# Two-input operations moved to VectorE and weight roundings to GpSimd in a fused attention and two-MoE kernel

## The chip, the cores and the metric

One Trainium2 chip, one core of it. The metric is the device time of the program in microseconds (us); for one core it is that core's time. Engines: TensorE (PE, with its weight loads as PEld), VectorE (DVE), ScalarE (ACT), GpSimd (POOL), and SyncE (SP), which issues all loads and stores.

## The reference

```python
def reference(**kwargs):
    attn_out = _attn_ref(**attn_kwargs)      # q, k, v: (4, 8, 576, 64); s: (4, 8, 576)
    B, H, S, D = attn_out.shape
    x = np.ascontiguousarray(attn_out.transpose(0, 2, 1, 3)).reshape(B * S, H * D)
    x = _moe_ref(x=x, **moe_kwargs)
    return _moe2_ref(x=x, **moe2_kwargs)
```

Attention is causal, with scores scaled by 1/8 and lowered by the running sum of max(s, 0) between key and query, then a softmax and the product with v. The first MoE is max(max(x w1, x w2), x w3) w_out with 2304 tokens, 512 columns in and out and 768 hidden ones. The second is ((x w_a) * (x w_b)) w_out with 1536 hidden columns. The second result is the output.

## The kernel before, in words

Every large product is made in three parts from split operands. An operand t is rounded into a high part (`rnd`, a copy into the type fp32r) and a low part t - high (`sub`, or `tt` with subtract); then high*high + high*low + low*high goes through TensorE. So each tensor that feeds TensorE costs one rounding (one input) and one subtraction (two inputs in SBUF) on ScalarE, VectorE or GpSimd; which engine does which is written out by hand at each place. In the code "A" is ScalarE, "V" VectorE and "P" GpSimd.

The stages overlap at their edges:

- **Attention and first MoE** (to some 520 us). Eight steps (4 batches, query rows up to 256 and above it), four pairs of heads in each. The first three steps ("plain") use unsplit operands for scores and values; the others split q, k, v and the probabilities. The products of the first MoE for one step (`moe1_units`, `gate` at L623 and `outp` at L650) are put between the attention pieces of later steps, so TensorE has one or the other. Its 24 weights of 128x512 come as 64-bit numbers and are made into fp32 by one ScalarE and three VectorE integer operations (`load_w`, L235 to L240), then split: rounding on ScalarE, subtraction on GpSimd (called at L244 and L245, recorded at L79 and L90). They are loaded over the first 1.8 steps. `vsplit` (v), `x_pair` (attention's result, Xh and Xl) and `gate` (hidden values, hh and hl) each end in a subtraction on GpSimd.
- **Second MoE, gates** (some 520 to 818 us). Both of its products use a seven-product scheme over 2x2 blocks: `a_side` and `b_side` make the sums of blocks and split seven operands each, and `Unit.prod` makes products 1, 2, 6, 5, 7, 4, 3 and adds them up from the PSUM banks X, Y and Z with ScalarE copies (L1087, L1091, L1093) and VectorE sums. Products 4 and 3 of a unit are made inside the next one (`emit`). There are 12 chunks of weights (`load_w2`, tiles wh and wl, each of two memory places) and 3 token blocks (`x2_part`, tiles xh and xl): 36 units of 42 matmuls of 384 columns. `load_w2` makes fp32 into wval, then does 4 VectorE sums, 7 ScalarE roundings and 7 GpSimd subtractions of 256 columns. `x2_part` for blocks 1 and 2 does 4 sums and 7 splits of 768 columns. The product a*b is made on VectorE for one half (`c21`) and on GpSimd for the other (`done`), and goes to HBM as hT.
- **Output** (from 818 us). Nine units of 256 tokens, 126 matmuls of 256 columns each (`outs`). `prep_wo` splits w_out once (tile wo; woh and wol of 128x1536: 4 sums, 7 roundings, 7 subtractions), `load_h` reads a block of hT into hraw with four loads, and `prep_h` does 4 sums and 7 splits of 128x768 into slots.

The order on each engine is made by a scheduler from the program's order and priorities: `tc.high_priority(n)` lets what stands in it come as if it stood n places earlier. Each engine then works its list in order, and so does SP with its loads and stores. Tiles lie in pools that are stacked from the left or the right end of SBUF; a pool that is laid over a released one waits for the old tiles' last readers, tile by tile. In the second MoE the left stack is wop (w_out, and before it the raw x of blocks 1 and 2), tmpA (raw weights, s, u), xr1 (x operands of block 1), wB (weights of odd chunks), xr2 (block 2), over the weights of the first MoE. In the output stage tmpB lies over tmpA, and lB (slots, l3, h7, l7, h4, l4, the second hraw) over the rest.

Of the kernel before, what the change touches and what calls it, by code (L numbers as in the profile page):

```python
# [27 lines left out]
def kernel(  # L28
# [44 lines left out]
    def f(ap):  # L73
        return ap.bitcast(F32)
# [148 lines left out]
    def load_w(raw, src, hi, lo):  # L223
# [5 lines left out]
        else:  # L229
# [13 lines left out]
            val = f(L)  # L243
        rnd("A", hi, val)  # L244
        sub("P", lo, val, f(hi))  # L245

# [115 lines left out]
    def vsplit(R, vn):  # L362

        Vs = ap_.tile([P, 5, 4, D], F32R, tag="Vs", bufs=1, name="Vs")
        nb = 5 if R else 2
        v_ = vn.rearrange("p b (h d) -> p b h d", h=2)
        hi, lo = Vs[:, :nb, 0:4:3, :], Vs[:, :nb, 1:3, :]
        rnd("P", hi, v_)
        sub("P", lo, v_, f(hi))
        return Vs  # L370
# [218 lines left out]
    def x_pair(R, p, pa, pb, Xh, Xl):  # L589
# [8 lines left out]
        rnd("A", Xh[:, p, :], xf[:, :n])  # L598
        sub("P", Xl[:, p, :], xf[:, :n], f(Xh[:, p, :]))

# [7 lines left out]
    def moe1_units(R, b, X):  # L608
# [4 lines left out]
        def gate(m, g):  # L613
# [19 lines left out]
            if g == 2:  # L633
                if m == 0:
                    st["hh"] = mp.tile([P, MF, N1], F32R, tag="hh", bufs=1, name="hh")
                    st["hl"] = mp.tile([P, MF, N1], F32R, tag="hl", bufs=1, name="hl")
                rnd("A", st["hh"][:, m, :n], hf)
                sub("P", st["hl"][:, m, :n], hf, f(st["hh"][:, m, :n]))

# [308 lines left out]
    def hilo(eng, hi, lo, src):  # L948
        rnd("A", hi, src)
        tt(eng, lo, src, f(hi), ALU.subtract)  # L950

# [74 lines left out]
    def load_x0():  # L1026
        for k in range(KH):
            q = rA.tile([P, 4, 1, TB], F32, tag="xt", bufs=1, name="xt")
            x2_part(0, k, k + 1, q, "PV")

# [12 lines left out]
    wop = lpool("wop")  # L1043
    xt12 = wop.tile([P, 2, 4, KH, TB], F32, tag="wo", name="xt12")
    tmpA = lpool("tmpA")
    rawp.append(tmpA)
    xr[1] = lpool("xr1")
    wpool[1] = lpool("wB")
# [54 lines left out]
    def gates(c, sb):  # L1103
# [20 lines left out]
        def done(t):  # L1124
            tt("P", t[1], t[0], t[1], ALU.mult)
            nc.sync.dma_start(hT[c * P : (c + 1) * P, t0 : t0 + TB], t[1])
# [38 lines left out]
    for n, (c, sb) in enumerate(order):  # L1165
        extra = []
        if n < 2:
            extra.append(lambda n=n: x2_part(n + 1, 0, KH, xt12[:, n], "VP"))
        done_c = [cc for cc in range(MF2) if (cc, NSB - 1) in order[:n]]
# [9 lines left out]
    xr[2].release()  # L1179
    wpool[1].release()  # L1180
    xr[1].release()
    tmpA.release()
    xr[0].release()
# [14 lines left out]
    hraw = [rB2.tile([P, MF2, 2 * P], F32, name="hraw0")]  # L1198
    wo_tiles(rB2, ("h1", "l1", "h2", "l2", "h3"))
    tmpB = lpool("tmpB")  # L1200
    obs = [tmpB.tile([P, DM], F32, name=f"ob{i}") for i in range(6)]
    tmpB.tile([P, 256], F32, name="pad2")
    lB = lpool("lB")
    slots = [lB.tile([P, KO, P], F32R, name=f"slot{i}") for i in range(18)]
    wo_tiles(lB, ("l3", "h7", "l7", "h4", "l4"))
    hraw.append(lB.tile([P, MF2, 2 * P], F32, name="hraw1"))
    NSLOT = len(slots)

    def prep_wo():
        eng = dict(zip((1, 2, 3, 6, 5, 7, 4), "VVPVVPV"))  # L1210
        b_side(
            [wo32[0][:, s] for s in range(4)],
            lambda i, q: hilo(eng[i], wot[f"h{i}"], wot[f"l{i}"], q),
        )

# [14 lines left out]
    def prep_h(j):  # L1230
        r = hraw[j % 2]
        hi, lo = {}, {}
        eng = dict(zip((1, 2, 4, 6, 5, 7, 3), "PVPVPVV"))

# [37 lines left out]
    NPR = len(porder)  # L1272
    with tc.high_priority(260):
        load_h(0)
    with tc.high_priority(160):
        prep_h(0)
    with tc.high_priority(100):
        prep_wo()
        load_h(1)
# [8 lines left out]

    lB.release()
    tmpB.release()  # L1290
    wop.release()
    ps_w.release()
# [89 lines left out]
```

## Time and profile before

| | |
|---|---|
| Runs | 973.07, 974.68, 978.18 us (median 974.68) |
| The profiled execution | 976.56 us, span 974.8 us |
| Mean granted TensorE clock | 0.986 of full speed |
| Busy share | TensorE 95%, weight loads 89%, VectorE 67%, ScalarE 49%, GpSimd 45% |
| Instructions of VectorE, ScalarE, GpSimd | 1349, 1068, 479 |

The span is what the trace covers; the profiled execution's own time is 1.8 us longer. Matmuls are pipelined, so a matmul's own duration is longer than the distance to the next one, and the rate of a stretch is read from its count. In a timeline line the columns are start, duration, engine, line and operation, written tile and read tiles, and in brackets how long the engine had been idle before and what ended that. Where a helper issues the operations, all have its line (L946 for `tt`, L79 to L86 for `rnd`, L90 for `sub`), so the tiles tell them apart.

### The profile page before, as it was taken

To read this page: it belongs to the slowest core of one execution; us is meant where nothing else is said; L and a number is where in the kernel's file an instruction comes from. 1 tells how busy PE (TensorE), PEld (TensorE's weight loads), DVE (VectorE), ACT (ScalarE), POOL (GpSimd) and SP (SyncE) were. 2 spreads that over 40 slices of the span, in tenths; PEclk is the share of its full clock that TensorE was granted. 3 is DMA by queue.
4 is the path that set the end of the run, shared out by engine and by line. 5 is a ranking of instruction groups with operands and counts; after the bars stand their busy time and mean duration, and the time that the engine had idled before them with its cause. 6 is when DMAs were issued, how large, how long until landed. Compare 5 with 4: busy or idle time off the path is not lost. (4 is left out here: it accounts for less than half of the span.)

```text
span 974.8 us, 17135 instructions
## 1 busy us (share of the span) xinstructions
PE 921.4 (95%) x6158; PEld 868.6 (89%) x6158; DVE 652.1 (67%) x1349; ACT 476.4 (49%) x1068; POOL 443.1 (45%) x479
## 2 busy tenths in 40 slices
PE   5999999999999999999998799898989997699998
PEld 4676689999999999999988698898989997699998
DVE  5899533686567766666574967766655567978774
ACT  4776643666556665566434434333333344345442
POOL 5676423355453455445364533333333435643431
PEclk9999999999999999999999799999999998899999
DMA  5655233212322141310325224444332133243531
GB/s 168 190 164 184 72 98 106 77 43 75 96 81 78 42 126 56 107 42 2 98 77 200 75 93 163 151 129 143 114 113 100 49 117 119 65 156 106 172 109 44
DMA packets 55213, 102.36 MB, mean 105 GB/s; under 512 B 5736, under 2 KB 39432, under 8 KB 55128
## 3 DMA queue, kind: packets, MB, share of 16 engines
q1 hardware_dynamic: 55128, 101.26, 33.0%
q8 instruction: 49, 0.80, 0.3%
q14 instruction: 36, 0.29, 0.1%
HBM read 77.29 MB, written 23.94 MB: 104 GB/s over the span
## 5 line engine op out<-in xcount | busy, mean ns | idle before, releaser
L623 PE MATMUL g<-Xh,hg 128*128 128x256 f32 (+1 forms) x576 | 172.1, 302 | 2.2 <-ACT hf L629 1.5
L623 PE MATMUL g<-Xl,hg 128*128 128x256 f32 (+1 forms) x576 | 172.7, 301 | 0.4 <-DVE Xl L90 0.4
L623 PE MATMUL g<-Xh,lg 128*128 128x256 f32 (+1 forms) x576 | 171.9, 300 | 0.0
L623 PEld LDWEIGHTS g<-Xh,hg 128*128 128x128 f32 x576 | 108.0, 189 | 5.3 <-ACT hf L629 1.7
L1058 PE MATMUL X<-xh,wh 128*128 128x384 f32 x288 | 100.5, 349 | 12.3 <-ACT s L1087 5.7
L623 PEld LDWEIGHTS g<-Xl,hg 128*128 128x128 f32 x576 | 109.0, 189 | 2.5 <-issue 1.0
L623 PEld LDWEIGHTS g<-Xh,lg 128*128 128x128 f32 x576 | 108.8, 189 | 2.3 <-issue 1.5
L946 POOL TENSOR_TENSOR wl<-wval,wh 128x256 fp32r<-128x256 f32 x84 | 69.6, 848 | 80.8 <-ACT wh L79 72.7
L1058 PE MATMUL X<-xl,wh 128*128 128x384 f32 x288 | 97.9, 340 | 0.0
L1058 PE MATMUL X<-xh,wl 128*128 128x384 f32 x288 | 97.8, 341 | 0.0
L946 POOL TENSOR_TENSOR slot<-hraw,slot 128x768 fp32r<-128x768 f32 x27 | 56.5, 2095 | 71.3 <-ACT slot L79 66.8
L946 POOL TENSOR_TENSOR u<-s,u 128x384 f32<-128x384 f32 x36 | 43.7, 1213 | 95.8 <-issue 63.9
L1058 PE MATMUL X<-woh,slot 128*128 128x256 f32 x432 | 83.7, 285 | 2.9 <-DVE slot L946 1.2
L79 ACT ACTIVATE slot<-hraw 128x768 fp32r<-128x768 f32 x63 | 52.3, 845 | 57.5 <-DVE hraw L946 48.1
L406 POOL TENSOR_SCALAR P<-P,rs 128x128 f32<-128x128 f32 (+2 forms) x80 | 47.1, 593 | 72.5 <-DVE rs L402 62.2
L1058 PEld LDWEIGHTS X<-woh,slot 128*128 128x128 f32 x432 | 69.4, 192 | 4.2 <-DVE slot L946 1.4
L1058 PEld LDWEIGHTS X<-xh,wh 128*128 128x128 f32 x288 | 54.7, 190 | 19.4 <-ACT s L1087 7.2
L946 DVE TENSOR_TENSOR hraw<-hraw 128x768 f32<-128x768 f32 x36 | 50.4, 1401 | 25.6 <-POOL slot L946 25.0
L632 DVE TENSOR_TENSOR hf<-g,hf 128x256 f32<-128x256 f32 (+1 forms) x96 | 43.5, 453 | 27.2 <-PE g L623 21.6
L1058 PE MATMUL X<-wol,slot 128*128 128x256 f32 x216 | 60.9, 283 | 0.0
L90 POOL TENSOR_TENSOR hl<-hf,hh 128x256 fp32r<-128x256 f32 (+1 forms) x48 | 41.5, 865 | 42.2 <-ACT hh L79 41.9
L650 PE MATMUL o<-hh,ho 128*128 128x256 f32 (+1 forms) x192 | 56.3, 302 | 1.7 <-DVE hf L632 1.3
(185 smaller groups left out, 2693.2 us busy)
## 6 DMA issues: line engine op xcount, KB each, us to landing
hT<-u SPq DMA_DIRECT2D x72, 192.0 KB
hraw<-hT SPq DMA_DIRECT2D x36, 384.0 KB
wraw<-in_moe_w_dram SPq DMA_DIRECT2D x18, 512.0 KB
wraw<-in_moe_w_out_dram SPq DMA_DIRECT2D x18, 512.0 KB
qvraw<-in_qv_dram SPq DMA_DIRECT2D x12, 640.0 KB
kraw<-in_kT_dram SPq DMA_DIRECT2D x24, 288.0 KB
wraw<-in_moe_w_a_dram SPq DMA_DIRECT2D x12, 512.0 KB
wraw<-in_moe_w_b_dram SPq DMA_DIRECT2D x12, 512.0 KB
```

The costliest lines, as they stand in the source:

```text
L79: nc.scalar.activation(o, i, AF.Copy, scale=scale)
L90: e.tensor_tensor(o, a, b, op=ALU.subtract)
L406: nc.gpsimd.tensor_scalar(pt[:, c0:c1], pt[:, c0:c1], rs[:, g : g + 1], 1.0, op0=ALU.mult, op1=ALU.mult,)
L623: nc.tensor.matmul(ps[:, :n], w[:, kk, :], x[:, kk, :], start=(i == 0), stop=(i == len(mm) - 1),)
L632: nc.vector.tensor_tensor(hf, ps[:, :n], hf, op=ALU.max)
L650: nc.tensor.matmul(ps[:, :n], w[:, c, :], x[:, m, :n], start=(i == 0), stop=(i == len(mm) - 1),)
L946: {"V": nc.vector, "P": nc.gpsimd}[e].tensor_tensor(o, a, b, op=op)
L1058: nc.tensor.matmul(ps[:, :n], w, x, start=(first and i == 0), stop=(i == len(mm) - 1), skip_group_check=not first,)
```

## The change

Subtractions go to VectorE at every place, and some roundings from ScalarE to GpSimd: all of those of the first and second MoE's gate weights, and a part of those of x, h and w_out. The a*b product of `done` goes to VectorE. The pools xr1 and tmpA swap places, with the raw tile the first in tmpA; l3 and twelve slots lie over xr1, the other slots with h7, l7, h4, l4 and the second hraw over wB and xr2. `prep_wo` is taken apart: its splits and sums are issued in four groups of falling priority, between them `prep_h(0)`.

```diff
@@ load_w (24 weights of the first MoE)
-        rnd("A", hi, val)
-        sub("P", lo, val, f(hi))
+        rnd("P", hi, val)
+        sub("V", lo, val, f(hi))
@@ vsplit (v)
         rnd("P", hi, v_)
-        sub("P", lo, v_, f(hi))
+        sub("V", lo, v_, f(hi))
@@ x_pair (attention's result)
         rnd("A", Xh[:, p, :], xf[:, :n])
-        sub("P", Xl[:, p, :], xf[:, :n], f(Xh[:, p, :]))
+        sub("V", Xl[:, p, :], xf[:, :n], f(Xh[:, p, :]))
@@ gate (hidden values of the first MoE)
                 rnd("A", st["hh"][:, m, :n], hf)
-                sub("P", st["hl"][:, m, :n], hf, f(st["hh"][:, m, :n]))
+                sub("V", st["hl"][:, m, :n], hf, f(st["hh"][:, m, :n]))
@@ second MoE: every split goes through hilo
     def hilo(eng, hi, lo, src):
-        rnd("A", hi, src)
-        tt(eng, lo, src, f(hi), ALU.subtract)
+        rnd(eng, hi, src)
+        tt("V", lo, src, f(hi), ALU.subtract)
@@ x of block 0, then of blocks 1 and 2
-            x2_part(0, k, k + 1, q, "PV")
+            x2_part(0, k, k + 1, q, "AP")
...
-            extra.append(lambda n=n: x2_part(n + 1, 0, KH, xt12[:, n], "VP"))
+            extra.append(lambda n=n: x2_part(n + 1, 0, KH, xt12[:, n], "AP"))
@@ memory of the second MoE
+    xr[1] = lpool("xr1")
     tmpA = lpool("tmpA")
+    tmpA.tile([P, WC, 2], I32, tag="raw", bufs=1, name="raw1")
     rawp.append(tmpA)
-    xr[1] = lpool("xr1")
@@ gates: the product a*b of the first half
         def done(t):
-            tt("P", t[1], t[0], t[1], ALU.mult)
+            tt("V", t[1], t[0], t[1], ALU.mult)
@@ memory of the output stage
+    lB1 = lpool("lB1")
+    wo_tiles(lB1, ("l3",))
+    slots = [lB1.tile([P, KO, P], F32R, name=f"slot{i}") for i in range(12)]
     tmpB = lpool("tmpB")
...
-    lB = lpool("lB")
-    slots = [lB.tile([P, KO, P], F32R, name=f"slot{i}") for i in range(18)]
-    wo_tiles(lB, ("l3", "h7", "l7", "h4", "l4"))
-    hraw.append(lB.tile([P, MF2, 2 * P], F32, name="hraw1"))
+    lB2 = lpool("lB2")
+    slots += [lB2.tile([P, KO, P], F32R, name=f"slot{i}") for i in range(12, 18)]
+    wo_tiles(lB2, ("h7", "l7", "h4", "l4"))
+    hraw.append(lB2.tile([P, MF2, 2 * P], F32, name="hraw1"))
...
-        eng = dict(zip((1, 2, 3, 6, 5, 7, 4), "VVPVVPV"))
@@ prep_h: engines of the seven splits
-        eng = dict(zip((1, 2, 4, 6, 5, 7, 3), "PVPVPVV"))
+        eng = dict(zip((1, 2, 4, 6, 5, 7, 3), "AAPAAPP"))
@@ order of the output preparation
-    with tc.high_priority(260):
+    with tc.high_priority(180):
         load_h(0)
-    with tc.high_priority(160):
+        sp_wo("A", 1, b11)
+        sp_wo("P", 2, b21)
+        tt("V", b11, b12, b11, ALU.subtract)
+        tt("V", b12, b22, b12, ALU.subtract)
+    with tc.high_priority(90):
+        sp_wo("A", 3, b22)
+        tt("V", b22, b22, b11, ALU.subtract)
+        tt("V", b21, b21, b22, ALU.subtract)
+    with tc.high_priority(70):
         prep_h(0)
-    with tc.high_priority(100):
-        prep_wo()
+    with tc.high_priority(40):
+        sp_wo("A", 6, b22)
+        sp_wo("P", 5, b11)
+    with tc.high_priority(10):
+        sp_wo("A", 7, b12)
+        sp_wo("P", 4, b21)
         load_h(1)
```

`sp_wo(eng, i, q)` is `hilo(eng, wot[f"h{i}"], wot[f"l{i}"], q)`, where b11, b12, b21 and b22 are the four blocks of wo.

## Rows read from the trace of the kernel before

**Rows 1.** Busy time by stretches: us, then PE, PEld, DVE, ACT, POOL busy (instructions), clock.

```profile
24.40:97.60 73.20, 70.08 (x416) 49.57 (x414) 66.39 (x157) 49.85 (x118) 51.02 (x47) 0.98 0.56 179
122.00:463.60 341.60, 341.60 (x2550) 334.63 (x2550) 211.02 (x632) 197.54 (x495) 158.51 (x220) 1.00 0.25 73
488.00:561.20 73.20, 62.64 (x352) 58.71 (x351) 54.32 (x67) 31.22 (x61) 38.74 (x30) 0.93 0.35 117
561.20:732.00 170.80, 159.69 (x886) 152.95 (x885) 113.85 (x206) 63.54 (x140) 61.41 (x70) 1.00 0.40 129
732.00:805.20 73.20, 73.20 (x419) 72.94 (x418) 42.83 (x64) 27.37 (x56) 28.23 (x31) 1.00 0.27 90
817.80:854.00 36.20, 23.82 (x150) 21.97 (x149) 34.22 (x21) 13.56 (x17) 25.44 (x9) 0.81 0.31 99
854.00:951.60 97.60, 97.60 (x830) 97.60 (x829) 74.08 (x72) 45.27 (x73) 38.75 (x20) 1.00 0.41 135
```

**Rows 2.** Timeline of TensorE and of ScalarE about 615 us.

```profile
615.50 0.44 PE L1058 MATMUL X<-xh,wh 128*128 128x384 f32 x1 [1.69 <-ACT s L1087]
...
614.67 0.42 ACT L79 ACTIVATE wh<-wval 128x256 fp32r<-128x256 f32 x1 [1.59 <-DVE wval L946]
```

**Rows 3.** Timeline of VectorE and of GpSimd about 385.8 us.

```profile
385.81 1.35 DVE L357 SCALAR_TENSOR_TENSOR QA<-qvraw,QA 64x640 fp32r<-64x640 f32 x1
...
385.75 0.73 POOL L86 TENSOR_SCALAR QA<-qvraw 64x640 fp32r<-64x640 f32 x1
```

**Rows 4.** VectorE: instructions on wval (min/median/max ns); timeline lines for three other widths.

```profile
L946 DVE TENSOR_TENSOR wval<-wval x48: 407/920/1883, 487.6 to 781.1; 128x256 f32<-128x256 f32 x48
...
26.86 0.68 DVE L240 SCALAR_TENSOR_TENSOR wraw<-wraw 128x512 int32<-128x512 int32 x1
...
797.77 1.74 DVE L946 TENSOR_TENSOR wol<-wo,woh 128x1536 fp32r<-128x1536 f32 x1
...
843.08 0.96 DVE L946 TENSOR_TENSOR slot<-hraw,slot 128x768 fp32r<-128x768 f32 x1
```

**Rows 5.** Handoff: TensorE's longest wait (us, times, longest), timeline, groups from 780 to 817.8.

```profile
PE Y L1058 <- DVE slot L946: 9.8, 2, 5.8
...
818.40 3.88 DVE L946 TENSOR_TENSOR slot<-hraw,slot 128x768 fp32r<-128x768 f32 x1
822.20 5.87 DVE L946 TENSOR_TENSOR wo<-wo 128x1536 f32<-128x1536 f32 x2
...
818.03 3.43 POOL L946 TENSOR_TENSOR wol<-wo,woh 128x1536 fp32r<-128x1536 f32 x1 [4.97 <-PE Z L1058]
...
L946 DVE TENSOR_TENSOR wol<-wo,woh 128x1536 fp32r<-128x1536 f32 x3 | 5.3, 1763 | 0.0
L946 DVE TENSOR_TENSOR wo<-wo 128x1536 f32<-128x1536 f32 x2 | 4.3, 2155 | 0.0
```

**Rows 6.** Groups by shape, GpSimd and VectorE, whole span: busy us, mean ns, idle before.

```profile
L946 POOL TENSOR_TENSOR wl<-wval,wh 128x256 fp32r<-128x256 f32 x84 | 69.6, 848 | 80.8 <-ACT wh L79 72.7 <-PE X L1058 5.6 <-DVE u L946 2.4
L946 POOL TENSOR_TENSOR slot<-hraw,slot 128x768 fp32r<-128x768 f32 x27 | 56.5, 2095 | 71.3 <-ACT slot L79 66.8 <-PE Z L1058 4.6
L946 POOL TENSOR_TENSOR u<-s,u 128x384 f32<-128x384 f32 x36 | 43.7, 1213 | 95.8 <-issue 63.9 <-DVE u L946 30.9 <-POOL wl L946 0.9
L90 POOL TENSOR_TENSOR lg<-wraw,hg 128x512 fp32r<-128x512 f32 x18 | 26.7, 1485 | 9.6 <-ACT hg L79 7.8 <-DMA kt<-ch 1.0 <-PE fj L458 0.5
L86 POOL TENSOR_SCALAR Vs<-qvraw 128x640 fp32r<-128x640 f32 x12 | 10.7, 889 | 4.2 <-PE pv L583 2.7 <-PE sj L449 1.4
L86 POOL TENSOR_SCALAR Vs<-qvraw 128x256 fp32r<-128x256 f32 x8 | 3.2, 404 | 5.9 <-PE pv L583 5.8
...
L240 DVE SCALAR_TENSOR_TENSOR wraw<-wraw 128x512 int32<-128x512 int32 x24 | 23.5, 981 | 0.1
```

**Rows 7.** Timeline of TensorE and of VectorE, first MoE to second.

```profile
543.10 0.44 PE L1058 MATMUL Z<-xl,wh 128*128 128x384 f32 x1 [2.54 <-DVE xl L946]
...
522.60 0.43 DVE L935 TENSOR_SCALAR wraw<-wraw 128x512 int32<-128x512 int32 x1 [10.76 <-DMA wraw<-in_moe_w_b_dram]
```

More of the change, by code (lines that the diff above doesn't have):

```diff
@@ L1180 @@
     wpool[1].release()
+    tmpA.release()
     xr[1].release()
-    tmpA.release()
     xr[0].release()
@@ L1202, with sp_wo @@
     tmpB.tile([P, 256], F32, name="pad2")
-    lB = lpool("lB")
-    slots = [lB.tile([P, KO, P], F32R, name=f"slot{i}") for i in range(18)]
-    wo_tiles(lB, ("l3", "h7", "l7", "h4", "l4"))
-    hraw.append(lB.tile([P, MF2, 2 * P], F32, name="hraw1"))
+    lB2 = lpool("lB2")
+    slots += [lB2.tile([P, KO, P], F32R, name=f"slot{i}") for i in range(12, 18)]
+    wo_tiles(lB2, ("h7", "l7", "h4", "l4"))
+    hraw.append(lB2.tile([P, MF2, 2 * P], F32, name="hraw1"))
     NSLOT = len(slots)
-    def prep_wo():
-        eng = dict(zip((1, 2, 3, 6, 5, 7, 4), "VVPVVPV"))
[L1211 to L1214, printed above, removed]
+    b11, b12, b21, b22 = (wo32[0][:, s] for s in range(4))
+    def sp_wo(eng, i, q):
+        hilo(eng, wot[f"h{i}"], wot[f"l{i}"], q)
     porder = list(range(NT // (2 * P)))
@@ L1287 @@
         prev[0].prod(i)
-    lB.release()
+    lB2.release()
     tmpB.release()
+    lB1.release()
     wop.release()
```

## The prediction

> **What bounds the kernel now.** I read first the busy time by stretches [rows 1]. TensorE is busy in all 341.60 us of the middle of attention, all 73.20 us of 732 to 805.2 and all 97.60 us of the output stage after 854: nothing on another engine can shorten those. The rest is where time can come from. Each loss is the time that the stretch's matmuls would need at the rate of a full stretch of the same stage. Gates of the second MoE, 561.2 to 732: 886 matmuls at 419 per 73.2 us need 154.8 us, and 16.0 us are lost. Handoff to the output stage, 817.8 to 854: 150 matmuls at 830 per 97.6 us need 17.6 us of 36.2, 18.6 lost, with the granted clock at 0.81 (part of it at the lower level, 1.2 GHz, behind the idle stretches). First MoE to second, 488 to 561.2: TensorE idle for 73.2 - 62.64 = 10.6 us, the clock at 0.93. And 24.4 to 97.6, where VectorE is busy 66.39 of 73.2 us: it loads and splits the first MoE's weights there.
>
> Then who waits. In the gates, one wait stands for most [rows 2]: TensorE stops for 1.69 us until ScalarE has copied s; ScalarE had stood 1.59 us in front of the rounding wh because VectorE's wval was late. ScalarE's queue is in order, so a weight rounding that nobody needs yet holds back an evacuation that TensorE needs.
>
> Why VectorE is late: it and GpSimd get in each other's way. The timeline has a two-input VectorE operation that takes 1.35 us beside a GpSimd rounding of 0.73 us that began 0.06 us before it [rows 3]. Alone, wval takes 0.407 us and its median is 0.920 [rows 4]; the 128x768 subtraction takes 0.96 alone and 3.88 beside GpSimd's wol, the two wo sums take 5.87 together where one 128x1536 operation alone takes 1.74 [rows 4, 5]. The excess is about the overlap: they take turns. Rows 3 also say that a one-input rounding on GpSimd takes its turn like a subtraction.
>
> **The change, part by part.** (1) Low parts (x minus rounded x) go to VectorE everywhere; roundings go from ScalarE to GpSimd for weights, and partly for x, h and w_out. The gates' product a*b goes from GpSimd to VectorE. (2) In the second MoE's memory order the x operands of block 1 swap places with the staging buffers. (3) The output preparation is issued in four steps of falling priority, and l3 moves to memory that falls free before the last gates.
>
> Prices [rows 6]. GpSimd's subtraction of 256 columns 0.848 us, of 512 1.485, of 768 2.095; its product of 384 1.213. A rounding there: 0.404 for 256 and 0.889 for 640, so about 1.26 ns a column (estimate): 0.73 for 512, 1.05 for 768, 2.0 for 1536. VectorE alone: 0.407, 0.68, 0.96 and 1.74 us for 256, 512, 768 and 1536 [rows 4]; 384 lies near 0.55 (estimate between the first and third). The Trainium skill (GPSIMD Engine Reference, section Engine selection) has one-input work on GpSimd at roughly line rate; at its 1.2 GHz that would be 1.3 us for 1536 (estimate) instead of 2.0, and the sum below about 2 us shorter. The rows decide here.
>
> Turns taken, per chunk of gate weights (three units, 21.9 us): GpSimd 7 x 0.848 + 3 x 1.213 = 9.6 us before, 7 x 0.404 = 2.8 after; VectorE gains 7 x 0.407 + 3 x 0.55 = 4.5. So the sum of both falls by 2.3 us only, but a turn is short (0.4 instead of 0.85 to 1.2), and ScalarE has no wh in front of its evacuations. VectorE goes from 113.85 / 170.8 = 67% to about 78%: 14.6 + 4.5 less 4 x (0.92 - 0.41) = 2.0 us of shorter wval, over 21.9.
>
> *Gates, 16.0 us lost.* The wait moves: a subtraction on VectorE now stands behind a 0.40 us GpSimd rounding, and behind it in VectorE's order are the sums out of Y and Z that free TensorE's banks. It is shorter than the 1.59 us of today, and there are as many. I take 6.5 us as gained, between -13 (nearly all of it goes) and +5 (VectorE at 78% lets its sums be late).
>
> *Handoff, 18.6 us lost.* TensorE's largest wait in the whole run is here: 9.8 us in two, for slot [rows 5]. VectorE's operations for it are eleven of 128x1536 (7 subtractions after the change, 4 sums) and eleven of 128x768: 11 x 1.74 + 11 x 0.96 = 29.7 us. Before 817.8 it had done three wol and two sums. The other sums need l3 done, and GpSimd's wol (of l3) starts only at 818.03, released by TensorE's last gate products [rows 5]. With l3 in earlier memory, four subtractions (1, 2, 3, 5) and all four sums can be done by then (8 x 1.74 = 13.9), leaving 15.8 us on VectorE and 2.0 + 3 x 1.05 = 5.2 us of GpSimd turns. Before, 4 x 1.74 + 8 x 0.96 = 14.6 on VectorE and two wol of 3.43 with three slots of 2.095 on GpSimd were left, 27.8 of turns. So 27.8 falls to between 15.8 and 21.0, taken at 19, 9 us less; less idle time saves some of the low clock, another 1 us. Taken -10, between -16 and 0. The first h block's four loads stand on SP behind the stores of hT, and a product of 0.55 us in place of 1.213 can only bring those forward; the second block's four are issued later and have a unit (126 matmuls, 14.8 us) to land. GpSimd issues no loads.
>
> *First MoE to second.* Two x blocks: before 16 VectorE operations of 0.96 and 6 GpSimd ones of 2.1, 28 us of turns; after 22 and six roundings of 1.05, 27.4. That is no relief. TensorE waits there for xl (2.54 us), and VectorE had stood idle for 10.76 us until w_b landed [rows 7]. The memory order puts the x operands over weights that are read earlier and the staging over later ones; the x loads still stand in SP's order behind the first MoE's last stores, and staging that comes free later can hold back w_b. Taken -1, between -8 and +6.
>
> *Early attention.* 24 weights: VectorE gains 0.68 each, 19 of them in the full stretch, 12.9 us; its integer operations lose part of their excess (0.981 against 0.68 [rows 4, 6], three kinds), and GpSimd's turn is 0.73 where it was 1.485, so about half: 8 us back. Net +5 against 6.8 us of slack; the weights may come a little late. Taken +1.5, between 0 and +10. In the middle of attention VectorE is busy 211.02 of 341.60 us [rows 1]; the 88 low parts of h, X and V in all of attention add 0.4 to 0.8 us each (estimate by width from rows 4), some 45 us. Behind such a subtraction, which waits for a rounding, stand softmax's minima and the maxima of g. TensorE is covered there by first-MoE products, and I cost it at nothing; if that cover is gone, a late low part costs its 0.4 to 0.8 us.
>
> *Output stage.* VectorE per unit: 11 x 0.96 and three sums of some 0.4 (256 columns, as wval alone) = 11.8 us of 14.8; it stays hidden.
>
> Sum: -6.5 - 10 - 1 + 1.5 = -16 us against this execution's 976.56 us (span 974.8), that is 960.6. The median of the runs shown, 974.68, is 1.9 us below this execution, so 958.7, said as 959.
>
> **Rivals.** *The waits vanish.* If the short turns free both transitions (handoff -16, gates -13, first to second -6, early 0), 35 us go: 940. For it: nearly every long VectorE operation here has a GpSimd one beside it. Against it: the sum of turns hardly falls. *Nothing is relieved.* Roundings on GpSimd take turns as in rows 3, the sums of turns are the 27.4 against 28 of above, and the handoff is started no earlier because its operations stand in the queues behind the last gates: gains of 2 us, 973. The Trainium skill (SBUF, section Who interferes with whom) speaks for it: a VectorE operation with two SBUF inputs and a GpSimd one that reads SBUF exclude each other for a whole instruction, and ScalarE, from which the roundings are taken, never waits for that. By that rule, the trace agrees. *VectorE becomes the bound.* Its place is the early stretch, where 90% is taken already: 12.9 us more with nothing back is 6.1 us over the slack; then the gates' sums late by 5 and the x blocks by 6, and the handoff's 6 won: 11 us more, 986. It decides if VectorE's busy share passes nine tenths where TensorE has no other work ready. Against it: the excess of today is real, and shorter GpSimd turns give some of it back.
>
> **How the numbers follow.** Forecast 0.48 (948 to 968), waits vanish 0.22, nothing relieved 0.14, VectorE the bound 0.16. A measurement of this kernel tells some 0.5% (4.9 us) from no change. Faster: 0.47 + 0.22 + 0.03 = 0.72; same: 0.01 + 0.11 + 0.01 = 0.13; slower: 0.15. The range goes from the vanishing waits to inside the slower case: 938 to 980.
>
> **What would show it.** Right: wval near 0.5 us, slot and wo on VectorE near 1 and 1.8 us, no wh on ScalarE, the wait for slot under 4 us, all four wo sums ended before the last gate product; 561 to 732 some 7 us shorter; 24.4 to 97.6 with VectorE over 70 us busy. Wrong: VectorE operations as long as today beside the roundings, TensorE's waits on s, u or xl as many with VectorE named, or idle TensorE in the middle of attention.

## The result, and the profile after

The changed kernel takes 959.34 us (median of 4 runs, 957.79 to 964.0), the one before 975.53 beside it (4 runs): ratio 0.9842, 95% interval 0.9818 to 0.9866. The profiled execution after took 960.47 us (span 958.7, mean granted clock 0.991). The forecast was 959.0.

First the busy time by stretches, with the columns of [rows 1]:

```profile
24.40:97.60 73.20, 71.70 (x422) 49.91 (x421) 63.20 (x180) 41.94 (x101) 35.51 (x41) 1.00 0.53 172
122.00:463.60 341.60, 340.99 (x2538) 333.74 (x2538) 242.63 (x696) 195.97 (x488) 94.22 (x144) 1.00 0.26 74
488.00:561.20 73.20, 64.11 (x366) 59.88 (x365) 59.48 (x104) 23.48 (x43) 22.54 (x23) 0.95 0.35 117
561.20:732.00 170.80, 166.35 (x938) 162.72 (x937) 133.10 (x292) 47.40 (x92) 28.45 (x56) 1.00 0.42 135
732.00:805.20 73.20, 72.17 (x420) 71.85 (x418) 51.79 (x87) 20.56 (x37) 10.47 (x17) 1.00 0.24 83
817.80:854.00 36.20, 30.09 (x230) 29.79 (x231) 27.89 (x33) 10.51 (x18) 7.64 (x8) 0.86 0.59 189
854.00:951.60 97.60, 97.14 (x824) 96.94 (x823) 73.41 (x86) 28.24 (x49) 18.86 (x18) 1.00 0.32 105
```

The stretches are fixed in time and the stages moved, so the gain is better placed by TensorE's own work. I took from each trace the start of the first gate matmul (128x384), of the 252nd and 1260th after it, and of the 126th output matmul (128x256) after the first; "end of first MoE" is the start of its last matmul:

| us | before | after | change | predicted |
|---|---|---|---|---|
| end of first MoE | 520.63 | 518.93 | -1.7 | +1.5 |
| boundary: first gate matmul to 252nd | 58.50 | 58.87 | +0.4 | -1 |
| gates: 252nd to 1260th | 192.49 | 184.70 | -7.8 | -6.5 |
| handoff: 1260th to 126th output matmul | 78.91 | 72.61 | -6.3 | -10 |
| from there to the end | 124.09 | 123.43 | -0.7 | 0 |

The groups by shape, which answer to [rows 4, 6] (busy us, mean ns, idle before), and the instructions on wval:

```profile
L946 DVE TENSOR_TENSOR wl<-wval,wh 128x256 fp32r<-128x256 f32 x84 | 35.5, 434 | 0.6 <-POOL wh L86 0.6
L86 POOL TENSOR_SCALAR wh<-wval 128x256 fp32r<-128x256 f32 x84 | 43.2, 524 | 207.8 <-PE Z L1059 134.8 <-DVE wval L946 42.0 <-PE o L650 12.4
L946 DVE TENSOR_TENSOR slot<-hraw,slot 128x768 fp32r<-128x768 f32 x63 | 62.8, 1015 | 21.3 <-POOL slot L86 18.3 <-ACT slot L79 2.9
L946 DVE TENSOR_TENSOR wo<-wo 128x1536 f32<-128x1536 f32 x4 | 7.0, 1747 | 0.0
L240 DVE SCALAR_TENSOR_TENSOR wraw<-wraw 128x512 int32<-128x512 int32 x24 | 16.5, 686 | 0.0
...
L946 DVE TENSOR_TENSOR wval<-wval x48: 406/414/618, 493.3 to 770.3; 128x256 f32<-128x256 f32 x48
```

The instructions of VectorE are back at their lengths alone: wval has a median of 0.414 us where it had 0.920, wo 1.75 where two took 5.87, L240 0.686 where it had 0.981. What waits now is mostly GpSimd: its rounding wh has a mean of 0.524 us, while the shortest takes 0.398.

At the handoff the timeline of VectorE has the four sums of w_out all among the gates (the last gate matmul starts at 814.59):

```profile
786.64 1.75 DVE L946 TENSOR_TENSOR wo<-wo 128x1536 f32<-128x1536 f32 x1
788.77 1.75 DVE L946 TENSOR_TENSOR wo<-wo 128x1536 f32<-128x1536 f32 x1
800.14 1.75 DVE L946 TENSOR_TENSOR wo<-wo 128x1536 f32<-128x1536 f32 x1
803.62 1.75 DVE L946 TENSOR_TENSOR wo<-wo 128x1536 f32<-128x1536 f32 x1
```

So the first output matmul comes at 798.38, 16 us ahead of the last gate one. But then TensorE waits for the second block: of the first unit's 126 matmuls it has made 54 when the next one in its order needs a slot of that block. Its waits from 780 to 870 us, its timeline, ScalarE's and SP's:

```profile
PE X L1059 <- ACT slot L79: 6.2, 1, 6.2
PE Y L1059 <- ACT slot L79: 2.8, 1, 2.8
...
821.09 0.58 PE L1059 MATMUL X<-woh,slot 128*128 128x256 f32 x1 [6.16 <-ACT slot L79]
...
820.19 0.84 ACT L79 ACTIVATE slot<-hraw 128x768 fp32r<-128x768 f32 x1 [6.51 <-DMA hraw<-hT]
823.82 0.84 ACT L79 ACTIVATE slot<-hraw 128x768 fp32r<-128x768 f32 x1 [2.78 <-DMA hraw<-hT]
...
814.78 0.37 SPq L1227 DMA_DIRECT2D hraw<-hT  x1
815.73 1.72 SPq L1227 DMA_DIRECT2D hraw<-hT  x3
```

The 9.8 us for slot of [rows 5] have become 6.2 + 2.8, and behind the slot roundings that end them stands the load of the second h block; the low clock behind it remains (0.86 in that stretch, 0.81 before).

### The profile page after: what moved, and what is told of

It reads as the page before. It is cut to its first block, busy times and chain, and to the rows that moved or that the text cites. A ratio compares the mean times of both kernels' runs of the same rounds, so it can differ in the third digit from the quotient of the medians.

```text
span 958.7 us, 17166 instructions
## 1 busy us (share of the span) xinstructions
PE 916.2 (96%) x6158; PEld 865.7 (90%) x6158; DVE 706.7 (74%) x1624; ACT 405.7 (42%) x918; POOL 250.6 (26%) x354
## 4 chain that ended last, share of the span: by engine, by line
PE 76%; DMA 10%; DVE 8%; issue 2%; ACT 1%; SPq 1%; POOL 1%; ACTq 0%; DVEq 0%; POOLq 0%
PE g L623 24%; PE X L1059 16%; PE Z L1059 8%; PE o L650 7%; PE pv L583 4%; PE Y L1059 4%; PE fpv L517 3%; PE t L546 3%; DMA wraw<-in_moe_w_b_dram 2%; PE f L458 2%; DVE u L946 1%; PE s L413 1%; PE s L414 1%; DMA wraw<-in_moe_w_out_dram 1%; DMA wraw<-in_moe_w_a_dram 1%
## 5 line engine op out<-in xcount | busy, mean ns | idle before, releaser
L86 POOL TENSOR_SCALAR wh<-wval 128x256 fp32r<-128x256 f32 x84 | 43.2, 524 | 207.8 <-PE Z L1059 134.8
L406 POOL TENSOR_SCALAR P<-P,rs 128x128 f32<-128x128 f32 (+2 forms) x80 | 49.9, 629 | 133.6 <-DVE rs L402 97.4
L946 DVE TENSOR_TENSOR slot<-hraw,slot 128x768 fp32r<-128x768 f32 x63 | 62.8, 1015 | 21.3 <-POOL slot L86 18.3
L86 POOL TENSOR_SCALAR slot<-hraw 128x768 fp32r<-128x768 f32 x27 | 28.1, 1041 | 127.9 <-DVE hraw L946 50.2
L79 ACT ACTIVATE slot<-hraw 128x768 fp32r<-128x768 f32 x36 | 30.4, 848 | 69.1 <-DVE hraw L946 37.1
L397 ACT ACTIVATE P<-P,nm 128x128 f32<-128x128 f32 (+2 forms) x80 | 46.5, 582 | 27.1 <-DVE nm L390 18.7
L1059 PEld LDWEIGHTS X<-xl,wh 128*128 128x128 f32 x288 | 54.2, 188 | 2.1 <-DVE xl L946 2.1
```

What stands on the lines that cost most here:

```text
L79: nc.scalar.activation(o, i, AF.Copy, scale=scale)
L86: nc.gpsimd.tensor_scalar(o, i, scale, 1.0, op0=ALU.mult, op1=ALU.mult)
L397: nc.scalar.activation(pt[:, c0:c1], pt[:, c0:c1], AF.Exp, bias=first, scale=-1.0, accum_out=sm[:, g : g + 1],)
L406: nc.gpsimd.tensor_scalar(pt[:, c0:c1], pt[:, c0:c1], rs[:, g : g + 1], 1.0, op0=ALU.mult, op1=ALU.mult,)
L946: {"V": nc.vector, "P": nc.gpsimd}[e].tensor_tensor(o, a, b, op=op)
L1059: nc.tensor.matmul(ps[:, :n], w, x, start=(first and i == 0), stop=(i == len(mm) - 1), skip_group_check=not first,)
```

## The experiments

All kernels are the changed one with the edit shown. "Gates" and "handoff" are the distances of the table above. Five of the kernels have in the gates the changed kernel's engines and its order of TensorE's products (attn_old, memory_old, order_old, h1_early, h1_early_prio); with the changed kernel itself their single profiles give gates of 180.9 to 184.7 us, and the end of the first MoE lies between 517.0 and 522.6 in all runs. So a difference under 4 us in the one or the other is not read from single profiles. The handoff of these, apart from memory_old, is 71.2 to 72.6. An edit of engines can also make the scheduler put TensorE's products in another order: of the 1008 matmuls between the 252nd and the 1260th, 586 stand elsewhere in the kernel before than in the changed one, 286 in w2_old, 524 in w2_round_act, 540 in mult_pool and in mult_pool_act, 506 in act_all and in best. extra_pool has w2_round_act's order, and mult_pool_act has mult_pool's.

| kernel | median us | ratio to before, 95% | boundary | gates | handoff |
|---|---|---|---|---|---|
| w2_old | 967.75 | 0.9897 to 0.9949 | 60.3 | 189.6 | 72.2 |
| w2_round_act | 956.44 | 0.9791 to 0.9837 | 58.2 | 180.1 | 73.0 |
| mult_pool | 972.04 | 0.9951 to 1.0008 | 63.1 | 192.5 | 72.6 |
| mult_pool_act | 967.14 | 0.9912 to 0.9945 | 60.2 | 191.1 | 73.8 |
| extra_pool | 966.42 | 0.9897 to 0.9949 | 59.3 | 185.0 | 77.0 |
| attn_old | 958.95 | 0.9812 to 0.9876 | 60.4 | 183.9 | 72.3 |
| memory_old | 963.13 | 0.9862 to 0.9907 | 58.6 | 182.8 | 76.0 |
| order_old | 958.01 | 0.9812 to 0.9852 | 58.9 | 182.8 | 71.9 |
| h1_early | 956.89 | 0.9799 to 0.9838 | 58.3 | 180.9 | 72.3 |
| h1_early_prio | 957.35 | 0.9800 to 0.9871 | 58.3 | 183.0 | 71.2 |
| act_all | 955.27 | 0.9780 to 0.9840 | 54.8 | 180.4 | 73.1 |
| best | 954.45 | 0.9761 to 0.9804 | 54.4 | 182.0 | 72.1 |

**1. Where the gates' gain comes from.** Three kernels undo one edit of the gates each, a fourth two of them.

w2_old:
```diff
-        rnd("P", hi, src); tt("V", lo, src, f(hi), ALU.subtract)   # gate weights only
+        rnd("A", hi, src); tt("P", lo, src, f(hi), ALU.subtract)
```


> The changed kernel with one edit undone: the gate weights of the second MoE are rounded on ScalarE and subtracted on GpSimd, as before; all else stays changed. If the gates' gain comes from this edit (short turns, and no rounding wh in front of ScalarE's copies), the distance from the 252nd to the 1260th gate matmul goes from 184.7 us back to 190 to 192.5, wval on VectorE from 0.46 back to 0.8 us or more, and the time to 964 to 967. If the gates' gain comes from the other edits there (the product a*b on VectorE, the x operands' memory), the distance stays within 2 us of 184.7 and the time within 2 us of 959.3.

w2_round_act:
```diff
-            lambda i, q: hilo("P", hi[:, i - 1], lo[:, i - 1], q),
+            lambda i, q: hilo("A", hi[:, i - 1], lo[:, i - 1], q),
```


> The changed kernel with the roundings of the gate weights on ScalarE again, the subtractions staying on VectorE, so that GpSimd has no part in these weights. Theory of the turns (VectorE was late because GpSimd's long subtractions excluded it, and ScalarE was late only through VectorE): wval stays under 0.5 us, and gates 252 to 1260 stay within 2 us of 184.7; 957 to 961. Rival, the queue of ScalarE (a rounding ahead of the copies of s holds them back whoever subtracts): 190 us or more, TensorE waits for s again for over 4 us in 561 to 732, and the time is 964 or more.

mult_pool:
```diff
-            tt("V", t[1], t[0], t[1], ALU.mult)
+            tt("P", t[1], t[0], t[1], ALU.mult)
```


> The changed kernel with the product a*b of the first half on GpSimd again (36 instructions of 1.2 us instead of some 0.55 on VectorE). If turns cost what they did before, VectorE's operations beside it lengthen and the gates take 1 to 3 us more (185.7 to 187.7 from the 252nd to the 1260th matmul): 960 to 963. Rival: there is slack for them on VectorE (78% busy) and GpSimd, and nothing changes by more than 1 us. Second rival: VectorE is relieved by the 36 products, and the gates are 1 to 2 us shorter.

mult_pool_act has both of the last two edits.

> Roundings of the gate weights on ScalarE and the product a*b of the first half on GpSimd, everything else as changed: GpSimd has nothing but that product in the gates. Compared with the run that has those roundings on ScalarE and the product on VectorE (956.4 us, gates 252 to 1260 in 180.1 us) it tells why the product on GpSimd cost 12 us when the roundings were there too. Theory of the in-order queue (the product stands on GpSimd behind a rounding that waits for its memory place or for wval, so s and u come free late and ScalarE's copies wait for it): with no rounding ahead the loss is gone, gates within 2 us of 180.1 and 956 to 959. Theory of the turns (a two-input instruction of 1.1 us on GpSimd shuts VectorE out): gates 186 to 192 us and 963 to 969, with VectorE's wval again over 0.55 us.

Groups of w2_old from 561 to 772 us:

```profile
L946 POOL TENSOR_TENSOR wl<-wval,wh 128x256 fp32r<-128x256 f32 x63 | 53.5, 882 | 148.6 <-ACT wh L79 148.6
L946 DVE TENSOR_TENSOR wval<-wval 128x256 f32<-128x256 f32 x36 | 26.3, 731 | 1.0
```

The same of w2_round_act:

```profile
L946 DVE TENSOR_TENSOR wl<-wval,wh 128x256 fp32r<-128x256 f32 x70 | 27.7, 416 | 1.2 <-ACT wh L79 1.1
L946 DVE TENSOR_TENSOR wval<-wval 128x256 f32<-128x256 f32 x40 | 16.6, 415 | 0.0
L940 DVE SCALAR_TENSOR_TENSOR wo<-wraw 128x256 int32<-128x256 int32 x24 | 9.0, 414 | 0.0
L946 DVE TENSOR_TENSOR u<-Z,u 128x384 f32<-128x384 f32 x56 | 30.7, 552 | 26.3 <-ACT u L1094 21.1 <-PE Z L1059 5.3
```

And of mult_pool_act:

```profile
L946 POOL TENSOR_TENSOR u<-s,u 128x384 f32<-128x384 f32 x26 | 28.1, 1083 | 178.1 <-DVE u L946 172.4 <-issue 5.6
L946 DVE TENSOR_TENSOR wl<-wval,wh 128x256 fp32r<-128x256 f32 x63 | 33.4, 557 | 0.2 <-ACT wh L79 0.2
L940 DVE SCALAR_TENSOR_TENSOR wo<-wraw 128x256 int32<-128x256 int32 x24 | 12.3, 552 | 0.0
L946 DVE TENSOR_TENSOR u<-Z,u 128x384 f32<-128x384 f32 x54 | 29.4, 552 | 16.1 <-ACT u L1094 13.5 <-PE Z L1059 2.4
```

With the subtraction on GpSimd again, wval goes back up to 0.73 us, and 8.4 of the 16.2 us are gone, 4.9 of them in the gates of the profile. This is the first theory's side, with wval below its 0.8 us, gates just below its 190 and a time just above its 967. With the product there, 12.7 are gone: 36 instructions of 1.1 us cost more than all 84 subtractions, in both with TensorE's products reordered as well. Both effects together would be 21 us of a gain of 16, so they are not additive: either kind of two-input work on GpSimd brings back half of the loss or more. My expectation for the product (1 to 3 us) was far off.

The roundings, on the other hand, need no GpSimd. Back on ScalarE they cost nothing (956.4 against 959.3, intervals overlapping), wl and wval are at 0.416 and 0.415, and TensorE's whole waits in 561 to 732 are 2.2 us. So the rival of ScalarE's queue falls, and with it a part of my own reason: a wh in front of ScalarE's copies does no harm while wval is in time. By this it was late because VectorE was.

mult_pool_act settles that the product doesn't lose its time behind GpSimd's roundings: there are none, and the gates still take 191.1 us. wl and the w_out conversions of VectorE lengthen by a third in the mean (0.557 and 0.552), though GpSimd works in only 23.89 us of the 175 from 580 to 755; wval stays at 0.414, against the expectation. The sums that take one operand from PSUM (u<-Z) stay at 0.552 in both.

The mean hides what happens. Two timeline lines of GpSimd in mult_pool_act, each with the wl beside it:

```profile
668.20 1.07 POOL L946 TENSOR_TENSOR u<-s,u 128x384 f32<-128x384 f32 x1 [2.03 <-DVE u L946]
668.32 1.24 DVE L946 TENSOR_TENSOR wl<-wval,wh 128x256 fp32r<-128x256 f32 x1
...
620.90 1.07 POOL L946 TENSOR_TENSOR u<-s,u 128x384 f32<-128x384 f32 x1 [4.96 <-DVE u L946]
620.69 0.41 DVE L946 TENSOR_TENSOR wl<-wval,wh 128x256 fp32r<-128x256 f32 x1
```

The wl that starts behind the product ends only after it; the one that starts before it keeps its length. So it is throughout: from 561 to 772 us, the 15 instructions of wl, wval and the w_out conversions that start behind a product take 1.228 to 1.243 us, the 16 that start before one 0.406 to 0.420. In the changed kernel 32 of them start behind a GpSimd rounding, and take 0.519 in the mean. So a one-input rounding shuts VectorE out too, but for a tenth of a microsecond.

**2. Turns by themselves.** Is it the turns, or that the product comes later? extra_pool adds to w2_round_act work whose result nothing reads.

```diff
                 tt("V", s1, ps[:, :n], s1, ALU.add)
+                if n == TB:
+                    for _ in range(2):
+                        tt("P", scr, s1[:, : n // 2], s1[:, n // 2 :], ALU.mult)
```


> The kernel with the gate weights' roundings on ScalarE (956.4 us; gates 252 to 1260 in 180.1 us, GpSimd empty there), plus work that nobody needs: in every gate unit GpSimd multiplies the two halves of s into a scratch tile, twice, 128x192 each, right after s is complete and some 5 us before s is needed for anything else. It adds work that no result depends on. With the product a*b on GpSimd the gates took 191.1 us. Theory of the turns (a two-input instruction on GpSimd shuts VectorE out, wherever it stands): VectorE's wl and wo conversions lengthen as they did there (0.557 and 0.552 us against 0.416 and 0.414), gates 185 to 192, time 961 to 968. Theory of the latency (the product on GpSimd is later by its own 1.1 us, so s and u come free late): gates within 2 us of 180.1, time 955.5 to 958.5.

Its groups from 561 to 772 us:

```profile
L946 POOL TENSOR_TENSOR scr<-s 128x192 f32<-128x192 f32 x57 | 50.2, 881 | 166.2 <-DVE s L946 163.2
L946 DVE TENSOR_TENSOR wl<-wval,wh 128x256 fp32r<-128x256 f32 x70 | 31.5, 470 | 0.3 <-ACT wh L79 0.2
```

10 us more for work that no instruction waits for: that turns cost time here is shown. In the gates, where TensorE's order is that of w2_round_act, they cost 4.9 us (180.1 to 185.0, more than the 3.8 by which equal gates lie apart). At the handoff it is 4.0, but there TensorE's order differs too. wl has 0.470 us, not the 0.557 of the expectation. GpSimd is busy longer here than with the product (50.2 us against 28.1), and the gates lose less than half of the 11.0 us that the product cost.

What the gates follow is neither GpSimd's busy time nor VectorE's, but what VectorE loses behind GpSimd. I summed, between the 252nd and the 1260th matmul, how much longer than the shortest of its kind each VectorE instruction took that started while a GpSimd one ran: none in w2_round_act, act_all and best (gates of 180.1 to 182.0 us), 3.3 to 3.7 us in the changed kernel and the five with its gates (180.9 to 184.7), 8.8 in extra_pool (185.0), 14.5 in w2_old (189.6), 14.8 in mult_pool_act (191.1), 16.6 in mult_pool (192.5) and 16.8 before (192.5). This is agreement over fourteen kernels, not a test: the product is also later by its 1.1 us, so s and u come free later (ScalarE's copy of s waits 13.2 us in all for the product in 561 to 732), and mult_pool_act has 297 of the 1008 matmuls in other places than w2_round_act. How the 11 us divide among these stays open. A third buffer for s and u would tell; it was not tried.

**3. The early edits.**

```diff
-        rnd("P", hi, val); sub("V", lo, val, f(hi))      # load_w
+        rnd("A", hi, val); sub("P", lo, val, f(hi))
-        sub("V", ...)                                    # vsplit, x_pair, gate
+        sub("P", ...)
```


> The changed kernel with the four edits of attention and first MoE undone (roundings of the 24 weights on ScalarE and their subtraction on GpSimd; subtraction of v, x and h on GpSimd); the second MoE and the output stay changed. The last first-MoE matmul was at 520.6 us before and is at 518.9 after. If these edits gave those 1.7 us (shorter turns in the early stretch), it goes back to 520 to 521, the time to 960.5 to 962. Prediction's view (they cost 1.5 us there and something else won 3): 516 to 517.5, and 956 to 958. If they do nothing: within 0.5 us of 518.9.

958.95 against 959.34: these four edits are worth nothing that a run can show. The first MoE's last matmul is at 517.0, which is where my prediction's view had it, but that end lies anywhere from 517.0 to 522.6 among all runs, so it supports none of the three views. The stretch from 24.4 to 97.6 us of attn_old, to be held against the first row of after:

```profile
24.40:97.60 73.20, 71.26 (x418) 50.63 (x417) 65.42 (x160) 50.46 (x117) 49.86 (x47) 1.00 0.53 179
```

VectorE does 20 instructions more there after the change and is busy for less time (63.20 us against 65.42): what it took over, it got back in shorter integer operations.

**4. The handoff: memory, order, load.** memory_old undoes both memory edits, order_old the order of the preparation.

```diff
@@ memory_old
-    xr[1] = lpool("xr1")                  # ahead of tmpA
-    lB1 = lpool("lB1"); l3 and slots 0 to 11 in it, ahead of tmpB
+    xr[1] = lpool("xr1")                  # behind tmpA
+    lB = lpool("lB"); all slots, l3, h7, l7, h4, l4, hraw1 in it, behind tmpB
@@ order_old
-    four groups at 180, 90, 40, 10, prep_h(0) at 70, load_h(1) at 10
+    load_h(0) at 260; prep_h(0) at 160; all of w_out, then load_h(1), at 100
```


> The changed kernel with both memory edits undone (staging under the x operands of block 1; all of the output's slots, l3 and the second hraw over the late memory), the new order of the output preparation kept. The handoff, from the 1260th gate matmul to the 126th output matmul, took 78.9 us before and 72.6 after. Theory that the memory of l3 decides (the sums of w_out need l3 done, which waits for the last gate products): the first output matmul comes after the last gate one again, the handoff goes back to 77 to 79 us, and the time to 964 to 966. Theory that priority and engines decide: handoff within 1.5 us of 72.6, 958 to 961.

> The changed kernel with the new memory, but the output preparation issued as before: first load_h, then prep_h, then all of prep_wo at one priority, then the second load_h. If the four groups of falling priority are part of the handoff's gain, it takes 74 to 79 us from the 1260th gate matmul to the 126th output matmul (72.6 after) and the time is 961 to 966, with gates possibly 1 to 3 us longer because the preparation comes earlier among them. If memory alone gives the gain, within 1.5 us of 72.6 and of 959.3.

Without the memory edits the handoff is 3.4 us longer (76.0 against 72.6, and 71.2 to 72.3 in the others), and as the memory theory said the first output matmul comes after the last gate one again (803.83 and 803.66). The median is 3.8 us longer (963.13 against 959.34, intervals overlapping); the two profiled executions differ by 0.4 only, since memory_old's gates came out 1.9 shorter. 3.4 is less than the 4.4 to 6.4 expected; the other 2.9 us of the handoff's gain stay when both memory edits are undone, and so belong to the engines of the splits or to the order. The order gives nothing beside the new memory: 958.01. That the 2.9 belong to the engines follows by elimination; no run undoes the engines of the output's splits alone.

Then the second block's load, first by memory alone, then by its place in SP's order too.

```diff
@@ h1_early
-    slots 12 to 17, h7, l7, h4, l4, hraw1
+    slots 12 to 15, a pad of 2 KB, hraw1, slots 16 and 17, h7, l7, h4, l4
@@ h1_early_prio, besides
+    with tc.high_priority(90):
+        load_h(1)                         # ahead of prep_h(0)
```


> The changed kernel with the second h block's memory put where the x operands of the first four products lay (free some 17 us earlier), instead of where those of the last ones lay; loads in the same order. In the profile after, TensorE's largest waits of the run (6.2 and 2.8 us) are for slots of the second h block, whose four loads start at 814.8 to 815.7 us. If that load is what is late after the change, they start at 807 to 809, these two waits fall under 2 us together, and the time is 953 to 956. Rival, VectorE is full there anyway (27.89 of 36.2 us between 817.8 and 854): the waits move to another operand of VectorE, and the time is 957.5 to 960.

> The changed kernel with the second h block's memory over the early operands of block 2, as in the run before, and its four loads issued ahead of prep_h(0). In that run only the first of the four started early (behind the store at 803.3), the other three stood on SP behind the next store at 811.8, and the waits for slots stayed at 5.2 and 2.1 us. If the loads are what is late, all four start within 2 us behind the earlier store, the two waits fall under 3 us together, and the handoff (72.6 in the changed kernel) to 67 to 70: 952 to 954.5. Rival, VectorE's or ScalarE's order is what is late (the sums of h for the second unit stand behind w_out's): handoff 71.5 to 73, 956 to 958.

In h1_early only the first load was early; the others stood behind the store of a product that VectorE finished late. Its time, 956.89, lies between the two forecasts and can't be told from the changed kernel's. In h1_early_prio all four start at 804.94, 10 us earlier than in the changed kernel by the clock and 7 us earlier by the gates (the 1260th matmul is at 759.97 and 762.65). SP's timeline, TensorE's waits from 780 to 870, and VectorE's timeline:

```profile
804.94 2.02 SPq L1229 DMA_DIRECT2D hraw<-hT  x4
...
PE X L1059 <- DVE slot L946: 4.9, 1, 4.9
PE X L1059 <- ACT slot L79: 2.3, 1, 2.3
...
815.62 3.91 DVE L946 TENSOR_TENSOR wol<-wo,woh 128x1536 fp32r<-128x1536 f32 x2
819.45 0.95 DVE L946 TENSOR_TENSOR slot<-hraw,slot 128x768 fp32r<-128x768 f32 x1
820.32 0.54 DVE L946 TENSOR_TENSOR u<-s,u 128x384 f32<-128x384 f32 x1
820.79 2.68 DVE L946 TENSOR_TENSOR slot<-hraw,slot 128x768 fp32r<-128x768 f32 x3
```

The load is out of the way, and the handoff is 71.2 us instead of 72.6. The waits sum to 7.2 instead of 9.0, and the largest now names VectorE: two wol stand ahead of the slots that TensorE needs, and in the timeline VectorE has no gap from 795 to 829 us. So the load theory falls. By what the handoff gained (1.4 us, where the other kernels with this memory lie between 71.9 and 72.6), the load was the last to end by little more than a microsecond at most; behind it VectorE's list was full, as the rival had it.

**5. GpSimd empty, and all of it together.** act_all is w2_round_act with the roundings of x, h and w_out on ScalarE too; best is act_all with h1_early_prio.

```diff
-  x2_part(..., "AP");  prep_h "AAPAAPP";  sp_wo("P", ...) for 2, 5 and 4
+  x2_part(..., "A");   prep_h "AAAAAAA";  sp_wo("A", ...) for all
```


> The kernel with the gate weights' roundings on ScalarE, and now all other roundings of the second MoE too (x, h, w_out): GpSimd does nothing from the second MoE on. Theory of the turns for the boundary (six roundings of x lengthened beside VectorE, up to 6 us for two): first gate matmul to the 252nd 55 to 57 us instead of 58.2, and the handoff 1 to 2 us shorter: 952 to 955. Rival: at the boundary VectorE is bound by its own work (23.7 of 24.4 us busy), and ScalarE's queue takes the roundings before the copies that TensorE needs: 956 to 958, or up to 3 us slower with waits for ScalarE at the output's start.

> The two changes that may add up, together: all roundings of the second MoE on ScalarE (955.3 us by itself) and the second h block's memory over early operands with its loads ahead of prep_h(0) (957.4 by itself, handoff 71.2 us, with VectorE busy without a gap from 795 to 829 us, two wol subtractions of w_out ahead of the slot that TensorE waits for, and GpSimd roundings beside them). Theory: the handoff is bound by VectorE's own work plus the turns that GpSimd's roundings take, so with GpSimd empty and the loads early it falls to 69 to 71 us, and the time to 951 to 953.5. Rival: VectorE's own work alone bounds it, the loads and the turns don't matter there: handoff 72 to 73.5 as with ScalarE's roundings alone, 954.5 to 956.

The groups of the x blocks from 519 to 565 us, in the changed kernel:

```profile
L946 DVE TENSOR_TENSOR xl<-xt,xh 128x768 fp32r<-128x768 f32 x14 | 15.1, 1080 | 2.1 <-ACT xh L79 1.4 <-POOL xh L86 0.7
L86 POOL TENSOR_SCALAR xh<-xt 128x768 fp32r<-128x768 f32 x6 | 10.6, 1775 | 11.4 <-DVE xt L946 7.1 <-ACT wraw L934 2.8 <-DMA xt<-x2T 1.5
```

In act_all, with the stretch that answers to the third of [rows 1]:

```profile
L946 DVE TENSOR_TENSOR xl<-xt,xh 128x768 fp32r<-128x768 f32 x14 | 13.2, 948 | 0.5 <-ACT xh L79 0.5
...
488.00:561.20 73.20, 66.16 (x390) 63.12 (x389) 57.02 (x107) 34.40 (x68) 0.00 (x0) 0.98 0.37 122
```

At the boundary the roundings on GpSimd did cost: xh took 1.775 us for work of some 0.83 (a slot rounding of that shape in the timeline of h1_early_prio), and a low part can't start before it. Without them the boundary is 54.8 us (54.4 in best) instead of the 58.2 of w2_round_act, and 390 matmuls stand in the stretch instead of 371; part of this can be TensorE's order, which differs from w2_round_act's in 89 of those 252 places. The handoff gained nothing from it (73.1 against 73.0), against that expectation, and the time, 955.27, lies between the two forecasts, 1.2 us below w2_round_act with intervals overlapping. Both also lose something: from the 126th output matmul to the end act_all and best take 124.6 us, the changed kernel and the other runs 123.3 to 123.7. TensorE's last eight units are as long as elsewhere; the 1.2 us come after the last matmul, where SP waits longer for a store, 2.77 us instead of 1.58. Why is open.

best takes 954.45 us (5 runs, 952.1 to 955.37), ratio 0.9783, its interval all below the changed kernel's. Between act_all and best no difference can be told. Its handoff, 72.1 us, is the rival's, its time just below the rival's. But the rival's reason, VectorE's own work, is not what the trace shows. The stretch in best, TensorE's longest wait from 780 to 870 us, and ScalarE's timeline:

```profile
817.80:854.00 36.20, 35.55 (x287) 35.55 (x288) 25.36 (x33) 14.46 (x25) 0.00 (x0) 0.94 0.41 135
...
PE X L1059 <- ACT slot L79: 4.3, 1, 4.3
...
811.85 0.84 ACT L79 ACTIVATE slot<-hraw 128x768 fp32r<-128x768 f32 x1 [6.34 <-PE Z L1059]
812.60 2.84 ACT L79 ACTIVATE woh<-wo 128x1536 fp32r<-128x1536 f32 x2
815.35 0.83 ACT L79 ACTIVATE slot<-hraw 128x768 fp32r<-128x768 f32 x1
```

The longest wait ends with ScalarE's rounding of a slot, which stands behind two roundings of w_out, and these behind one that waited 6.34 us for TensorE. The waits that name VectorE sum to 2.2 us. So with GpSimd empty it is ScalarE's list that ends last here; the order of that list was not tried.

## Why the prediction was right, and where it was not

*The time* came out within 0.4 us, the split less well: the handoff gave 3.7 us less than I said and the boundary 1.4 less, the end of the first MoE 3.2 more and gates and output 2.0 more. The first MoE's end lies 5.6 us apart among the runs, so that part of the balance is luck.

*Gates, -6.5: -7.8 measured.* The size was right as far as single profiles tell (with the five other kernels that have these gates it is up to 11.6), and so was VectorE's share (133.10 / 170.8 = 78%), and no PE wait for s is left above 0.7 us. The reason was half right. That a short turn of GpSimd hurts little holds: what starts behind one takes 0.519 us instead of 0.413, behind a product 1.237. "ScalarE has no wh in front of its evacuations" was no cause: w2_round_act puts them back and loses nothing. And the a*b product, 3.6 of the 9.6 us of GpSimd's turns per chunk in my sum, cost more when put back than the seven subtractions. That sum, 2.3 us less per chunk, was the wrong measure: it counts the work of both engines, while VectorE loses only what it stands behind GpSimd's instructions, 16.8 us of the gates before and 3.7 after.

*Handoff, -10: -6.3 measured.* The steps with l3 and the four sums happened as said, and memory_old shows that this memory gives 3.4 us. The step that failed is that the second block's loads "have a unit (126 matmuls, 14.8 us) to land". Only 54 of the first unit's matmuls stand ahead of the first one that needs the second block, and all 54 ran among the last gates, so that unit was no cover: TensorE waited 6.2 us for the second block soon after the last gate matmul. Nor would an earlier load have made up the difference: with it (h1_early_prio) 4.9 of the 7.2 us of waits name VectorE, and with GpSimd's roundings on ScalarE besides (best) 4.3 of 7.1 name ScalarE. VectorE's subtractions were in the sum (15.8 us), but I set against them only the first unit's need, not the second block's eleven operations that follow at once. "The wait for slot under 4 us" was wrong for the same reason.

*First to second MoE, -1: +0.4.* The working (28 against 27.4 us of turns, no relief) was right. act_all shows that the other choice, roundings on ScalarE, was worth some 3.4 us more there (58.2 to 54.8, TensorE's order changed too): no GpSimd rounding stands beside xl, which takes 0.948 us instead of 1.080. My price of 1.05 us for a GpSimd rounding of 768 columns fits neither case: it is 0.83 alone and was 1.775 in the mean here, waits included.

*Early attention, +1.5.* "VectorE over 70 us busy" was wrong: 63.20, less than before. I took 8 us as what its integer operations get back, and L240 alone, 19 times 0.37 us shorter in that stretch (1.055 to 0.686), gives 7 of them; with L236 and L237 (0.28 and 0.13 us shorter each) it is some 14, against 12 added by 17 subtractions of 0.717. In the time nothing shows either way (attn_old).

*The rivals.* "Nothing is relieved" rested on the rule that the two engines exclude each other. The rule holds, as the profile after has it: whichever starts second waits, and here that was mostly the rounding. The Trainium skill (SBUF — State Buffer, section Who interferes with whom) adds that who blocks is decided by the order of issue, and that a VectorE instruction with one SBUF input doesn't contend outside the 2-port modes. The traces agree: in mult_pool_act 1.228 to 1.243 us behind a product and 0.406 to 0.420 ahead of one, and u<-Z, from PSUM and SBUF, at 0.55 us beside GpSimd or alone (in the kernel before 0.549 for the 22 that started behind a GpSimd instruction, 0.552 for the 42 alone). What made the rival wrong is that a rounding holds VectorE up for a tenth of a microsecond, and that one which itself waits delays little: TensorE waits for wh once from 561 to 732, for 1.1 us. "VectorE becomes the bound" named the wrong place: not the early stretch but the boundary (VectorE busy 23.67 us of the 24.4 from 536.8 on) and the handoff, as parts of a gain.

## What to carry to other kernels

Keep two-input work off GpSimd where VectorE is near its limit, even if GpSimd is idle most of the time: here 36 products of 1.1 us in a GpSimd that was 14% busy cost 11 us, and multiplications that nobody reads cost 10. Don't judge this by busy shares: VectorE was busier after the change (78% instead of 67% from 561 to 732) and the gates were shorter. Sum what VectorE's instructions lose behind GpSimd's. Where a rounding can stand on ScalarE, test that before GpSimd: here VectorE lost nothing to it (wl and wval at 0.416 and 0.415 us). When the profile names a late load, see what else ends just before it: moving the load 7 us forward gained about one at most, because VectorE's list came next.

## What was not expected of the hardware

A few long waits can hide in a mean. In mult_pool_act wl is longer by 0.14 us in the mean and so are the w_out conversions, 12 us together; but it is 15 instructions that lose some 0.82 us each, because they start behind a GpSimd product of 1.07 us, and all the others lose nothing. One-input roundings on GpSimd, 35.1 us of them in the same window of the changed kernel, lengthened wl by 0.014 us (0.430 against 0.416) and wval by 0.046: they are short, and most of the waiting fell on the roundings, which started second.
